# Low weight words scaled on GpSimd, a shorter warm-up and new priorities in a planned attention and two-MLP kernel

## The chip, the cores and the metric

The kernel runs on one core of a Trainium2 chip. The metric is the device time of one execution in microseconds (us). PE is TensorE, ACT is ScalarE, DVE is VectorE, POOL is GpSimd, and SP is the engine whose queue issues nearly all DMAs.

## What is computed

Windowed attention with a distance bias, then two MLPs on its 2304 output rows. All inputs are float32, but the four weight matrices reach the kernel as 64-bit numbers in 32-bit halves.

```python
scores = scale * q @ k.T + slopes * -|rel|     # 4 batches, 8 heads, 576 rows, head 64
scores = where(0 <= rel < 128, scores, -1e9)
x = softmax(scores) @ v                        # -> (2304, 512)
h = x @ w_in                                   # (2304, 2048)
P = a0 + a1*h + a2*h**2 + a3*h**3
Q = 1 + |b0|*|h| + |b1|*h**2
x = (P / (Q + 1e-6)) @ w_out                   # (2304, 512)
h = x @ w2_in
out = (h * sigmoid(h)) @ w2_out
```

## The kernel before

**A planner orders everything.** `plan_kernel` records each piece of work with `Plan.op`: a priority, an engine or a table of engines with a cost in ns for each, the tiles it reads and writes, and a function that issues it. `Plan.schedule` then plays the engines forward in time: of the pieces that are ready it takes the one of lowest priority, on the engine of its table where it can start first, and keeps tile buffers, DMA landings and the port that it lets POOL and DVE's SBUF operations share. The functions are called in the order of the planned start times; on the chip each engine runs its own part of that order and waits by semaphores. `OPT` holds the options (engines allowed for each kind of piece, offsets of priorities, numbers of buffers), and `SHIFTS` adds an offset to the priorities of stretches of pieces, by number.

**Attention.** The 18 tiles of 128 rows are cut into five blocks of 4, 4, 3, 4, 3 tiles. For each block and each of four pairs of heads a group (`group`, from L648 on) computes scores (L698) for two tiles at a time, a masked copy and bias and row minimum on DVE (L704, L711), exponentials on ACT (L715), a normalising product (L734, option `norm`, for block 0 `norm0`), transposes (L754), two masked halves `ph` of the transposed probabilities (on DVE at L799 and L803, or copied by ACT and masked by POOL at L785 and L786 in block 0; options `mk00` to `mk03` say which for the two heads of each group of block 0: `d` DVE, `p` POOL), and the product with v (L831). The result is split into a high word `xh` by a rounding copy and a low word `xl` by a subtraction (DVE at L855, or ACT and POOL at L851; options `xl00` to `xl03`).

**First MLP.** 80 steps of (block, 128 columns of 2048). A step computes `h` with 12 matmuls (L889 to L891: high by high, high by low, low by high, for four tiles of 128 rows of weights), the rational function on ACT and DVE (L905 to L934, the last one DVE's L934), its split into `gh` and `gl`, and 12 matmuls into four accumulators `acc` (L958 to L960).

**Weights.** Each of the 64 raw tiles (16 for each of the four matrices, 512 KB) goes through `raw_weight`: a load by SP into one of three buffers (L549); an ACT operation that rescales the top words (L561); the scaling of the low words in place, unsigned integers with a stride of two words, by 2^-32 × 7.499 (L564, option `shift`, on ACT in the kernel before); and a DVE shift and OR that joins the words (L567). `weight` then makes the high word (L466 or L474) and the low word (L485). First-MLP input weights are also written to DRAM (`spill`, L597, from the queue of option `sq`) and loaded again for later blocks (L606).

**Second MLP.** Three groups of six tiles by a fast matrix scheme with seven products; its weights are combined by `prep` (sums and splits, written to DRAM by SP, L1122) while the first MLP runs, and streamed back (L1133). Its matmuls are L1233 to L1235 and L1299 to L1301, all with 384 columns.

**The start.** `k_ident` makes an identity matrix on POOL; PE multiplies it with itself (`spin`, L511) `warm` times, and more often where the planner sees PE idle for over 300 ns before the first MLP runs. SP loads the first two tiles of k and q (L636), half of a table (L524), the next tiles, the other half, and so on.

Of the kernel before, what the change touches and what calls it, by code (L numbers as in the profile page):

```python
# [50 lines left out]
    'tabs': 'pool',  # L51
    'stb': 3,
    'strb': 3,
    'wpro': 0.256,
    'dS': -1.52,
    'dT': 0.037,
    'dA': 0.149,
    'dm': 0.366,
    'look': 0.451,
    'pw': -0.72,  # L60
    'pwo': -0.374,
    'dg': -5.616,
    'lead': 2.536,
    'slk': 0,
    'warm': 6,
    'fill': 0.6,
    'fillmin': 300.0,
    'fs': 10,
    'ob': 3,
    'pl': -0.721,  # L70
    'vlead': -1.233,
    'qlead': -1.974,
    'keen': 9999.0,
    'norm0': 'pool',
    'sq': 'act',
    'xq': 'sp',
    'mk': 'pd',
    'mk00': 'dd',
    'mk01': 'dp',
    'mk02': 'dd',  # L80
    'mk03': 'dd',
    'xl00': 'd',
    'xl01': 'd',
    'xl02': 'p',
    'xl03': 'd',
    'alt': 0,
    'gh0': 'act|dve',
    'gl0': 'pool',
    'la': 8.921,
    'lb': 302.617,  # L90
    'dm2': 1.231,
    'sums': 'pool',
    'fhi': 'act|pool',
    'flo': 'dve|pool',
# [1 line left out]
    'xsum': 'dve|pool',  # L96
    'xfh': 'act|pool',
    'xfl': 'pool',
    's1': 'act',
    'tsum': 'pool',  # L100
    'th': 'act|dve',
    'tl': 'dve|pool',
    'tlead': 1.016,
    'hlead': -0.505,
    'oq': 'sp',
    'pw2': 511.696,
    'rw2': 25.851,
    'pwo2': 1331.915,
    'rwo2': 14.569,
    'xlead': -0.854,  # L110
    'slead': 0.691,
    'shift': 'act',
    'tail': 1,
}

SHIFTS = [
# [6 lines left out]
]  # L125


# [44 lines left out]
class Plan:  # L172
# [11 lines left out]
    def op(self, prio, eng, cost, fn, reads=(), writes=(), after=(), dma=False):  # L184
# [6 lines left out]
        o.port = {e for e in o.alts if e == "pool" or e == "dve" and not o.banks}  # L191
        o.deps, o.allocs = set(after), []
        o.dma = dma or eng == "sp"
        o.lag = max([LAG.get(t[0], 0.0) for t in writes], default=0.0) if o.dma else 0.0
        for t in list(reads) + list(writes):
            key, reg = t[:2], t[2:]
            if key not in self.tile_ops:
# [191 lines left out]
def plan_kernel(ctx, tc, qn, kn, vp, table, w1, wo1, w2, wo2, out):  # L389
# [124 lines left out]
        T[("h", "spin")] = h_p.tile([P, 512], F32, tag="h", name="spin")  # L514
        spin(OPT["warm"])

    pl.op(-98, "pe", 427 * OPT["warm"], first_spin, reads=[("ident", 0)], writes=[("h", "spin")])
    pl.spin = spin

    late = []  # L520

    def late_consts():
        for part, cols in ((0, slice(0, 3 * P)), (1, slice(3 * P, 6 * P + 16))):
            pl.op(-91.0 + 0.5 * part, "sp", 700, lambda cols=cols: nc.sync.dma_start(tab_all[:, cols], table[:, cols]), writes=[("tab", part)])  # L524
        for part in range(2):
            for h in range(H):
                pl.op(-70 + 0.1 * h + 10 * (h // 2) + 25 * part, do_copy("act" if h + part == 0 else OPT["tabs"], 2 * P,
                      lambda h=h, part=part: (tabs[:, h, 2 * part:2 * part + 2], tab[:, 4 * part:4 * part + 2]), scale=-8.0 * 2.0 ** -(h + 1)), 0, None,
                      reads=[("tab", part)], writes=[("tabs", h, part)])
        late.append(("na", 0))  # L530
        late.append(("ab", 0))
        pl.op(-3, "dve", 80, lambda: nc.vector.tensor_scalar(out=na, in0=coef[:, 0:4], scalar1=-1.0, scalar2=None, op0=ALU.mult),
              reads=[("tab", 1)], writes=[("na", 0)])
        pl.op(-3, "act", 200, lambda: nc.scalar.activation(out=ab, in_=coef[:, 4:6], func=AF.Abs), reads=[("tab", 1)], writes=[("ab", 0)])
# [8 lines left out]
    def raw_weight(name, f, src, p, load_p):  # L543
# [12 lines left out]
        if wide:  # L556


            top = lambda: T[rk][:, :, 1].bitcast(F32)
            low = lambda: T[rk][:, :, 0].bitcast(U32)  # L560
            pl.op(p - 0.6, "act", c_act(NR) + 45, lambda: nc.scalar.activation(out=top(), in_=top(), func=AF.Prelu, scale=2.0 ** -112, alpha=2.0 ** 32),  # L561
                  reads=[rk + (1,)], writes=[rk + (1,)])
            pl.op(p - 0.5, any_of(OPT["shift"], {
                "act": (c_act(NR) + 45, lambda: nc.scalar.activation(out=low(), in_=low(), func=AF.Copy, scale=LOW_SCALE)),  # L564
                "dve": (c_dve2x(NR), lambda: nc.vector.tensor_scalar(
                    out=low(), in0=low(), scalar1=29, scalar2=None, op0=ALU.logical_shift_right))}), 0, None, reads=[rk + (0,)], writes=[rk + (0,)])
            pl.op(p - 0.3, "dve", c_dve(NR), lambda: nc.vector.scalar_tensor_tensor(  # L567
                out=top().bitcast(U32), in0=top().bitcast(U32), scalar=3, in1=low(), op0=ALU.logical_shift_left, op1=ALU.bitwise_or),
                reads=[rk], writes=[rk + (1,)])
# [890 lines left out]
```

## Time and profile before

| | us |
|---|---|
| median of 3 runs | 869.5 (868.25 to 870.54) |
| the profiled execution | 869.16 |
| its span, first to last instruction | 867.3 |
| PE busy | 855.2 (99%) |
| DVE busy | 643.1 (74%) |
| POOL busy | 637.9 (74%) |
| ACT busy | 603.1 (70%) |

Busy times add up the time in which an engine had an instruction in work. The ends of matmuls are modelled and overlap the next ones, so PE's busy time does not say how much of it is needed; the distance between the starts of matmuls does. A row of a timeline gives the start, the duration, the engine and line, what is written and read, and in brackets how long the engine was idle before it and what released it. A line of the chain of waits gives the start, the time spent and what it was spent on.

### The profile page before, as it was taken

Reading aid. Unit: us, or ns where it says so; the run is one execution under the profiler, and the core shown is the slowest. Engines: PE = TensorE matmul, PEld = TensorE weight load, DVE = VectorE, ACT = ScalarE, POOL = GpSimd, SP = SyncE. Lnnn points to the kernel's source line nnn. Section 1 sums busy time; section 2 is a strip of 40 time slices with the busy share of each in tenths; the row PEclk is TensorE's granted clock in tenths of the full one; section 3 lists DMA queues with packets and bytes.
Section 4 is the critical chain, followed back from the end, with each engine's and each line's share of the span. In section 5 each row is a group of like instructions: output and inputs, shape, how many; then the busy total and the mean of one; then the engine's idle time right before and its main releaser. Section 6 shows DMA issues by size and latency. Waiting matters only on the chain.

```text
span 867.3 us, 15300 instructions
## 1 busy us (share of the span) xinstructions
PE 855.2 (99%) x5076; PEld 765.1 (88%) x5076; DVE 643.1 (74%) x1308; ACT 603.1 (70%) x1291; POOL 637.9 (74%) x613
## 2 busy tenths in 40 slices
PE   8989999999999999999999999999999999999998
PEld 6667778877788998777889999999999999999998
DVE  7899897789999898998889984357733477433652
ACT  6699997799888988887889984446434365344452
POOL 4778845666888897878899677479954599744884
PEclk9999999999999999999999999999999999999999
DMA  7746764586889887876797889898888888878884
GB/s 253 264 161 214 243 223 137 169 277 227 289 310 321 294 280 263 306 255 238 275 349 240 295 297 356 262 318 281 281 277 250 292 288 282 295 248 258 252 269 169
DMA packets 80462, 228.94 MB, mean 264 GB/s; under 512 B 8192, under 2 KB 17152, under 8 KB 80384
## 3 DMA queue, kind: packets, MB, share of 16 engines
q1 hardware_dynamic: 78080, 219.59, 76.2%
q10 hardware_dynamic: 2304, 8.39, 2.4%
q8 instruction: 40, 0.66, 0.3%
q14 instruction: 38, 0.31, 0.1%
HBM read 178.66 MB, written 49.28 MB: 263 GB/s over the span
## 4 chain that ended last, share of the span: by engine, by line
PE 82%; DVE 5%; ACT 4%; POOL 3%; DMA 3%; issue 2%; SPq 0%; ACTq 0%; POOLq 0%; DVEq 0%
PE acc L958 6%; PE h L889 6%; PE acc L960 6%; PE acc L959 6%; PE h L891 5%; PE h L890 5%; PE z_a L1233 4%; PE z_b L1300 4%; PE z_a L1234 4%; PE z_a L1235 4%; PE z_b L1301 4%; PE z_b L1299 4%; PE bank_atA L831 3%; PE bank_atA L698 2%; PE bank_atA L1233 1%
## 5 line engine op out<-in xcount | busy, mean ns | idle before, releaser
L485 POOL TENSOR_TENSOR xl_b<-g,xh_b 128x384 fp32r<-128x384 f32 x81 | 90.6, 1119 | 69.6 <-ACT xh_b L466 67.8
L466 ACT CAST xh_b<-g 128x384 fp32r<-128x384 f32 x162 | 83.0, 514 | 64.3 <-PE z_b L1301 42.0
L958 PE MATMUL acc<-gh,wo 128*128 128x512 f32 (+1 forms) x320 | 121.1, 378 | 0.0
L960 PE MATMUL acc<-gl,wo 128*128 128x512 f32 (+1 forms) x320 | 118.7, 371 | 0.1
L959 PE MATMUL acc<-gh,wo 128*128 128x512 f32 (+1 forms) x320 | 117.8, 368 | 0.0
L481 DVE TENSOR_TENSOR xl_b<-g,xh_b 128x384 fp32r<-128x384 f32 x87 | 87.3, 1014 | 30.3 <-ACT xh_b L466 29.1
L485 POOL TENSOR_TENSOR gl<-t,gh 128x512 fp32r<-128x512 f32 (+1 forms) x76 | 93.0, 1224 | 15.9 <-ACT gh L466 12.5
L385 ACT ACTIVATE g<-t_a 128x384 f32<-128x384 f32 x72 | 37.9, 526 | 75.2 <-DVE t_a L378 75.2
L485 POOL TENSOR_TENSOR g<-g,g 128x384 f32<-128x384 f32 x72 | 84.5, 1185 | 2.0
L889 PE MATMUL h<-xh,ws 128*128 128x512 f32 (+1 forms) x224 | 84.2, 376 | 0.4 <-DVE t L934 0.4
L891 PE MATMUL h<-xh,ws 128*128 128x512 f32 (+1 forms) x224 | 82.2, 367 | 0.0
L890 PE MATMUL h<-xl,ws 128*128 128x512 f32 (+1 forms) x224 | 82.1, 367 | 0.0
L958 PEld LDWEIGHTS acc<-gh,wo 128*128 128x128 f32 x320 | 60.1, 188 | 13.4 <-issue 5.6
L960 PEld LDWEIGHTS acc<-gl,wo 128*128 128x128 f32 x320 | 60.0, 188 | 9.5 <-POOL gl L485 1.5
L959 PEld LDWEIGHTS acc<-gh,wo 128*128 128x128 f32 x320 | 60.1, 188 | 6.7
L1233 PE MATMUL z_a<-xf,w2s 128*128 128x384 f32 x192 | 64.2, 335 | 0.0
L1235 PE MATMUL z_a<-xf,w2s 128*128 128x384 f32 x192 | 64.1, 334 | 0.0
L1234 PE MATMUL z_a<-xf,w2s 128*128 128x384 f32 x192 | 64.1, 334 | 0.0
L1299 PE MATMUL z_b<-xh_b,wo2s 128*128 128x384 f32 x192 | 64.1, 334 | 0.0
L1300 PE MATMUL z_b<-xl_b,wo2s 128*128 128x384 f32 x192 | 64.1, 334 | 0.0
L1301 PE MATMUL z_b<-xh_b,wo2s 128*128 128x384 f32 x192 | 64.1, 334 | 0.0
L715 ACT ACTIVATE e<-e,m 128x128 f32<-128x128 f32 x144 | 56.0, 392 | 7.6 <-DVE m L711 7.3
(207 smaller groups left out, 2701.9 us busy)
## 6 DMA issues: line engine op xcount, KB each, us to landing
w2s<-forms_w SPq DMA_DIRECT2D x84, 512.0 KB, 4.7
wo2s<-forms_wo SPq DMA_DIRECT2D x84, 512.0 KB, 4.6
ws<-sc SPq DMA_DIRECT2D x64, 512.0 KB, 4.4
raw_w<-in_w SPq DMA_DIRECT2D x32, 512.0 KB, 4.9
raw_wo<-in_wo SPq DMA_DIRECT2D x32, 512.0 KB, 4.9
forms_w<-st_w SPq DMA_DIRECT2D x24, 512.0 KB, 5.0
forms_wo<-st_wo SPq DMA_DIRECT2D x24, 512.0 KB, 4.9
sc<-w ACTq DMA_DIRECT2D x16, 512.0 KB, 5.2
```

Source lines behind the costliest of these rows:

```text
L485: nc.gpsimd.tensor_tensor(out=o, in0=a, in1=b, op=op)
L889: nc.tensor.matmul(o, lhsT=T[W][:, 0, c], rhs=xh, start=kt == 0, stop=False)
L890: nc.tensor.matmul(o, lhsT=T[W][:, 0, c], rhs=xl, start=False, stop=False)
L891: nc.tensor.matmul(o, lhsT=T[W][:, 1, c], rhs=xh, start=False, stop=kt == KD - 1)
L958: nc.tensor.matmul(a, lhsT=T[WO][:, 0, c], rhs=T[G1][:, :n], start=first_f, stop=False)
L959: nc.tensor.matmul(a, lhsT=T[WO][:, 1, c], rhs=T[G1][:, :n], start=False, stop=False)
L960: nc.tensor.matmul(a, lhsT=T[WO][:, 0, c], rhs=T[G2][:, :n], start=False, stop=last_f)
L1233: nc.tensor.matmul(o, lhsT=w(0, kt * P), rhs=x[:, 0, kt], start=st and kt == 0, stop=False, skip_group_check=True)
L1234: nc.tensor.matmul(o, lhsT=w(0, kt * P), rhs=x[:, 1, kt], start=False, stop=False, skip_group_check=True)
L1235: nc.tensor.matmul(o, lhsT=w(1, kt * P), rhs=x[:, 0, kt], start=False, stop=kt == 1, skip_group_check=True)
L1299: nc.tensor.matmul(o, lhsT=w(0, m * P), rhs=h, start=st and q == 0, stop=False, skip_group_check=True)
L1300: nc.tensor.matmul(o, lhsT=w(0, m * P), rhs=l, start=False, stop=False, skip_group_check=True)
```

## The change

Low words may now be scaled by POOL as well as ACT; the planner gives POOL 46 of the 64. The warm-up is three matmuls, not six, and is planned at 470 ns each. Spills go to SP's queue. The planner no longer adds a delay of its own after the first q, k, v and table loads, and takes more time for the table. Normalising in block 0 may go to DVE, several pieces get one more engine, the masks and low words of single groups of block 0 change engines, and the offsets of priorities and `SHIFTS` are new numbers throughout.

```diff
-    'warm': 6,
+    'warm': 3,
-    'vlead': -1.233,
-    'qlead': -1.974,
+    'vlead': 0.616,
+    'qlead': 0.725,
-    'norm0': 'pool',
-    'sq': 'act',
+    'norm0': 'dve|pool',
+    'sq': 'sp',
-    'mk00': 'dd',
-    'mk01': 'dp',
+    'mk00': 'pd',
+    'mk01': 'dd',
-    'xl00': 'd',
-    'xl01': 'd',
-    'xl02': 'p',
+    'xl00': 'p',
+    'xl01': 'p',
+    'xl02': 'd',
-    'gh0': 'act|dve',
-    'gl0': 'pool',
+    'gh0': 'act',
+    'gl0': 'dve|pool',
-    's1': 'act',
+    's1': 'act|dve',
-    'th': 'act|dve',
+    'th': 'act|dve|pool',
-    'shift': 'act',
+    'shift': 'act|pool',
...
 SHIFTS = [
...
-        o.lag = max([LAG.get(t[0], 0.0) for t in writes], default=0.0) if o.dma else 0.0
+        o.lag = max([LAG.get(t[0], 0.0) for t in writes if t[1] != 0], default=0.0) if o.dma else 0.0
...
-    pl.op(-98, "pe", 427 * OPT["warm"], first_spin, reads=[("ident", 0)], writes=[("h", "spin")])
+    pl.op(-98, "pe", 470 * OPT["warm"], first_spin, reads=[("ident", 0)], writes=[("h", "spin")])
...
-            pl.op(-91.0 + 0.5 * part, "sp", 700, lambda cols=cols: nc.sync.dma_start(tab_all[:, cols], table[:, cols]), writes=[("tab", part)])
+            pl.op(-91.0 + 0.5 * part, "sp", 1150, lambda cols=cols: nc.sync.dma_start(tab_all[:, cols], table[:, cols]), writes=[("tab", part)])
...
             pl.op(p - 0.5, any_of(OPT["shift"], {
                 "act": (c_act(NR) + 45, lambda: nc.scalar.activation(out=low(), in_=low(), func=AF.Copy, scale=LOW_SCALE)),
+                "pool": (c_pool_ts(NR) + 90, lambda: nc.gpsimd.tensor_scalar(out=low(), in0=low(), scalar1=LOW_SCALE, scalar2=1.0, op0=ALU.mult, op1=ALU.mult)),
```

The other numbers of `OPT` that change are offsets of priorities: `wpro`, `dS`, `dT`, `dA`, `dm`, `look`, `pw`, `pwo`, `dg`, `lead`, `pl`, `la`, `lb`, `dm2`, `tlead`, `hlead`, `pw2`, `rw2`, `pwo2`, `rwo2`, `xlead`, `slead`. `SHIFTS` has 60 entries in place of 37.

## Rows read from the trace of the kernel before

**Rows 1.** Busy time by stretch: PE, PEld, DVE, ACT, POOL, clock, DMA, GB/s.

```profile
0.00:57.00 57.00, 49.92 (x447) 36.59 (x447) 47.03 (x179) 41.55 (x135) 37.55 (x50) 1.00 0.71 239
57.00:520.00 463.00, 461.24 (x2647) 384.76 (x2648) 416.20 (x884) 406.26 (x849) 361.03 (x360) 1.00 0.76 260
520.00:867.30 347.30, 344.02 (x1985) 343.70 (x1983) 179.83 (x246) 155.28 (x308) 239.36 (x204) 1.00 0.84 274
```

**Rows 2.** The same view, of two stretches with matmuls of one width.

```profile
140.00:150.00 10.00, 10.00 (x46) 8.29 (x45) 7.88 (x15) 6.72 (x10) 5.38 (x6) 1.00 0.33 107
560.00:580.00 20.00, 20.00 (x117) 20.00 (x117) 9.23 (x15) 8.08 (x16) 11.41 (x12) 1.00 0.94 309
```

**Rows 3.** Timeline of PE: transposes, values, a wait for h, a scores block.

```profile
25.57 1.09 PE L754 MATMUL bank_acc<-ident,e 128*128 128x128 f32 x8
...
50.25 1.95 PE L831 MATMUL bank_atA<-ph,vh 128*64 128x256 f32 x20 [1.27 <-POOL ph L792]
...
54.52 0.50 PE L889 MATMUL h<-xh,w 128*128 128x512 f32 x1 [1.01 <-DVE t L934]
...
56.11 0.37 PE L698 MATMUL bank_atA<-kd,qd 64*64 64x192 f32 x1
...
56.92 0.50 PE L889 MATMUL h<-xh,w 128*128 128x512 f32 x1
```

**Rows 4.** Instructions of the spin line: duration ns min/median/max, first and last start.

```profile
L511 PE MATMUL spin<-ident x62: 275/275/582, 1.4 to 27.3; 128*128 128x128 f32 x62
...
L511 PE MATMUL bank_acc<-ident x38: 272/275/377, 30.7 to 53.2; 128*128 128x128 f32 x38
```

**Rows 5.** Timeline of the first 7 us, and the landing of k's loads up to 12 us.

```profile
1.17 0.42 SPq L636 DMA_DIRECT2D qd<-in_qn  x1
...
1.36 3.78 PE L511 MATMUL spin<-ident 128*128 128x128 f32 x16 [1.36 <-POOL ident masks.py:199]
...
4.47 0.42 ACT L466 ACTIVATE tabs<-tab 128x256 f32<-128x256 f32 x1 [2.46 <-DMA tab<-in_table]
...
5.07 0.57 PE L698 MATMUL bank_atA<-kd,qd 64*128 64x128 f32 x1
...
6.30 0.29 DVE L704 COPY_PREDICATED bank_atA<-tab,bank_atA 128x128 f32<-128x128 uint32 x1 [2.11 <-PE bank_atB L698]
...
DMA to landing us min/median/max: 2.2/4.1/8.3
```

**Rows 6.** The chain that ended last, in the first 62 us.

```profile
12.00 2.05 POOL e L734 x2
...
25.63 1.24 POOL ph L785
...
26.95 1.28 POOL ph L786
...
34.23 6.79 DMA raw_w<-in_w
...
43.80 0.56 ACT raw_w L564
```

**Rows 7.** DVE's joining of words: least/median/most; then its group (busy, mean ns).

```profile
L567 DVE SCALAR_TENSOR_TENSOR raw_w<-raw_w x32: 647/736/1404, 20.3 to 360.7; 128x512 uint32<-128x512 uint32 x32
...
L567 DVE SCALAR_TENSOR_TENSOR raw_w<-raw_w 128x512 uint32<-128x512 uint32 x32 | 26.2, 824 | 1.9 <-ACT raw_w L564 1.7
```

**Rows 8.** Instructions of the low-word scaling on ACT (32 more on raw_wo).

```profile
L564 ACT ACTIVATE raw_w<-raw_w x32: 647/672/703, 17.6 to 357.2; 128x512 uint32<-128x512 uint32 x32
```

**Rows 9.** Groups of POOL up to 520 us: busy, mean ns of one, idle before.

```profile
L485 POOL TENSOR_TENSOR w<-raw_w,w 128x512 fp32r<-128x512 f32 x16 | 21.4, 1338 | 0.9 <-ACT w L466 0.2
...
L474 POOL TENSOR_SCALAR wo<-raw_wo 128x512 fp32r<-128x512 f32 x11 | 7.6, 690 | 12.9 <-DVE raw_wo L567 12.9
```

**Rows 10.** Waits of DVE: us in total, times, longest us.

```profile
DVE t L930 <- ACT h L928: 19.5, 30, 2.5
```

**Rows 11.** Timeline of POOL and DVE at 28 us.

```profile
28.18 1.30 POOL L485 TENSOR_TENSOR w<-raw_w,w 128x512 fp32r<-128x512 f32 x1
...
28.40 1.11 DVE L726 TENSOR_SCALAR l<-l 128x8 f32<-128x8 f32 x1 [0.24 <-ACT e L715]
```

**Rows 12.** Spills on ACT's queue, and SP's waits before raw loads.

```profile
L597 ACTq DMA_DIRECT2D sc<-w x16: 326/326/362, 24.7 to 195.8; - x16
...
SPq L549 <- POOL w L485: 46.9, 15, 5.8
```

More of the change, by code (lines that the diff above doesn't have):

```diff
@@ L53 @@
     'strb': 3,
[L54 to L63, printed above, removed]
+    'wpro': 0.226,
+    'dS': -1.459,
+    'dT': 0.01,
+    'dA': 0.283,
+    'dm': 0.426,
+    'look': 0.312,
+    'pw': -0.595,
+    'pwo': -0.37,
+    'dg': -1.781,
+    'lead': 2.551,
     'slk': 0,
-    'warm': 6,
+    'warm': 3,
     'fill': 0.6,
@@ L69 @@
     'ob': 3,
-    'pl': -0.721,
-    'vlead': -1.233,
-    'qlead': -1.974,
+    'pl': -0.649,
+    'vlead': 0.616,
+    'qlead': 0.725,
     'keen': 9999.0,
-    'norm0': 'pool',
-    'sq': 'act',
+    'norm0': 'dve|pool',
+    'sq': 'sp',
     'xq': 'sp',
     'mk': 'pd',
-    'mk00': 'dd',
-    'mk01': 'dp',
+    'mk00': 'pd',
+    'mk01': 'dd',
     'mk02': 'dd',
     'mk03': 'dd',
-    'xl00': 'd',
-    'xl01': 'd',
-    'xl02': 'p',
+    'xl00': 'p',
+    'xl01': 'p',
+    'xl02': 'd',
     'xl03': 'd',
     'alt': 0,
-    'gh0': 'act|dve',
-    'gl0': 'pool',
-    'la': 8.921,
-    'lb': 302.617,
-    'dm2': 1.231,
+    'gh0': 'act',
+    'gl0': 'dve|pool',
+    'la': 7.958,
+    'lb': 108.335,
+    'dm2': 4.831,
     'sums': 'pool',
@@ L98 @@
     'xfl': 'pool',
-    's1': 'act',
+    's1': 'act|dve',
     'tsum': 'pool',
-    'th': 'act|dve',
+    'th': 'act|dve|pool',
     'tl': 'dve|pool',
-    'tlead': 1.016,
-    'hlead': -0.505,
+    'tlead': -0.003,
+    'hlead': -0.973,
     'oq': 'sp',
[L106 to L111, printed above, removed]
-    'shift': 'act',
+    'pw2': 30.726,
+    'rw2': 16.788,
+    'pwo2': 1188.783,
+    'rwo2': 3.36,
+    'xlead': -0.899,
+    'slead': 0.222,
+    'shift': 'act|pool',
     'tail': 1,
```

15 rows, old and new, of the table SHIFTS are left out of this document.

## Prediction

> **What bounds the kernel now.** I read the busy times by stretch first. They fall into three stages [rows 1]. From 520 us to the end PE is busy without a break, and DVE, ACT and POOL have half their time or more to spare but for POOL (239 of 347 us). Nothing that only relieves or loads those three can move the end of that stage: it is 2,016 matmuls of 384 columns one after another. From 57 to 520 us PE is again busy (461.2 of 463 us), but DVE (416), ACT (406) and POOL (361) are nearly full. From 0 to 57 us PE is busy for 49.9 us, partly with idle spins.
>
> How much of this is lost is worked out from the spacing of matmuls, since their modelled ends hide short pauses. Where only matmuls of 512 columns run, 46 are counted in 10 us with both edges in, which makes about 0.225 us each; with 384 columns 117 in 20 us make 0.172 us [rows 2]. By the code the first MLP has 48 steps of 24 matmuls with 512 columns and 32 steps of 24 with 384: 259 + 132 us. The second MLP takes 2,016 × 0.172 = 347 us. The attention of 72 tile pairs: a scores block of two tiles takes 56.92 - 56.11 = 0.81 us, so 72 × 0.4 = 29 us; a transpose about 0.12 us, 144 of them 17 us; the values 1.95 us for a group of four tiles and about three quarters of it for one of three, together 35 us [rows 3]. The sum is some 819 us, an estimate good to a few us. The span is 867.3 us, so some 48 us are not work. About 26 us of them lie in the first 57: the 100 spin records [rows 4], 16 at 0.23 us and the others at about 0.12, make some 14 us, and PE's waits and starts between them, such as the waits of about 1 us before 50.25 and 54.52 us [rows 3], most of the rest. Some 15 to 20 us are left for 57 to 520 us, as pauses of about 0.1 us where a block of matmuls begins. These two sums are all that the change can win from.
>
> **The start.** Six warm-up matmuls become three. The 16 spin records from 1.36 us on end when the first scores matmul starts at 5.07 us; by the code they are six warm-up matmuls and two fillers, of two records each. The first q was issued at 1.17 us, and the quickest landing of these loads took 2.2 us, so the data were there at about 3.4 us [rows 5]. Three warm-up matmuls fewer are six records of about 0.22 us, 1.3 us, so the scores can start at about 3.8 us. DVE's first operation on them then comes at about 5.0 us, after the table's landing (ACT's first use of it was released at 4.47 us), in place of 6.30 [rows 5]. That 1.3 us is the gain if nothing else is late, and nothing is gained if the next groups' q and k, which land as before, end the wait. The new leads for q, k and v (qlead -1.97 to 0.73, vlead -1.23 to 0.62) put those loads ahead of raw weights in SP's queue, which helps the groups and delays the weights. I take **-0.9 us**, between 0 and -1.3 and nearer the full gain because the chain passes from these spins straight into group 0. The later rise of TensorE's clock has a price: the first spins run at half the later rate (16 records in 3.78 us against 8 in 1.09 us at 25.57 of the same size [rows 3, 5]), which is the lower of 1.2 and 2.4 GHz although the column shows 1.00 there. If the rise comes later by the 1.3 us of spins that are gone, the work in it takes twice as long, at most +0.7 us; that end stays in the range.
>
> **The attention of block 0.** Normalising may now go to DVE too. On the chain it is 2.05 us at 12.00 [rows 6] for two POOL operations; the DVE scores operations around it are each 0.2 to 0.4 us, and a DVE product of 512 elements costs some 0.65 us by its nearest row (L567's least, 0.65 [rows 7]), 1.3 us for the pair: -0.7 us where DVE is free. Group 1's masks go from ACT and POOL to DVE: the two POOL pieces at 25.63 and 26.95 (2.5 us on the chain) become about 1.3 us: -1.2 us. Group 0's go the other way for one head, +1.2 us by the same prices, but beside the other head's masks on DVE, so I count half. Groups 0 and 1 get their low words from POOL (an extra ACT copy and 1.3 us of POOL), group 2 from DVE; for the price of two DVE operations saved and one added I count nothing, with ±1 us as bounds. Sum **-1.3 us**; bounds -3 and +2.
>
> **The shift.** Each low-word scaling on ACT takes 0.67 us, 0.56 us of it on the chain where operations stand back to back [rows 6, 8]. On POOL it does not exist in this trace. The nearest row is POOL's one-input copy from the same strided raw tile, 0.69 us; the far end is POOL's two-input operation, 1.34 us [rows 9]. I take 0.69 since the new operation has one input. So 46 of them take 46 × 0.56 = 26 us from ACT and put 32 us (up to 62) on POOL. In the first stage ACT is the chain without a break from 41 to 50 us, with one scaling in it, and POOL idles before 44 us: **-0.6 us**, or up to -1.7 with the two other scalings of that stretch. From 57 to 520 us ACT falls to about 383 of 463 us and POOL rises to about 390. What ends PE's pauses there is DVE's last operation of a step, and DVE in turn waits for ACT (19.5 us at L930 alone [rows 10]); with ACT 6% emptier I let these waits shrink by a tenth and a tenth of the 15 to 20 us go with them: -1.7 us.
>
> Against that stands DVE's wait for POOL. A DVE operation of 8 elements took 1.11 us at 28.40, until POOL's operation of 28.18 had ended [rows 11], and L567 takes 0.65 us at best, 1.40 at worst and 0.82 in the mean [rows 7]. The excess of 0.17 us over 64 of them is 11 us; with 9% more POOL work it grows by 1 us, some of it hidden: +0.5 us. Net for the stage **-1.2 us**. The Trainium skill says in "SBUF — State Buffer", Who interferes with whom, that GpSimd and DVE instructions with two SBUF inputs hold a shared port pair exclusively for a whole instruction, and that ScalarE waits for nobody. The two rows agree, and by that rule the move puts 32 us of new lock where ACT had none. Taken at full price it is the second rival below.
>
> **The rest.** Spills move from ACT's queue to SP: 16 issues of 0.33 us [rows 12], which overlap ACT's work now. SP already waits for the same POOL operation before a raw load (15 times, 46.9 us), so a spill beside it delays a load by 0.33 us: nothing, covered by load times of some 5 us. If a spill stood ahead of a load that was ready, the load would be late by SP's wait, up to 5.8 us [rows 12]; one such case reaching PE costs about 1 us. Splits and copies of the second MLP, which get POOL or DVE as a further choice, lie under a PE without gaps: nothing. In block 0 the high words of g leave DVE for ACT and the low words may come to DVE: one copy each way, inside the bounds that follow. The new priorities and shifts of whole stretches have no row. Their bounds are half of the pauses gone (-8 us) and five waits of the size before 54.52 (+5 us); I take 0 beyond what is counted.
>
> **Sum.** -0.9 - 1.3 - 0.6 - 1.2 = -4.0 us. The profiled execution took 869.16 us (span 867.3), 0.3 us under the median of 869.5. 869.2 - 4.0 = 865.2 us. About 0.3%, 2.6 us, is what a measurement here can tell from no change: below 866.9 is faster, above 872.1 slower.
>
> **Rivals.** (a) Hidden anyway: the first stage ends where weight loads (6.8 us for the one at 34.23 [rows 6]) and DVE (47 of 57 us) let it, and 57 to 520 us is matmul-bound to within 0.1 us pauses that come from semaphores and not from late engines. Then only a few tenths of the start remain: 868.9 us. For it: PE is 99.6% busy there; against it: the spins. Chance 0.25. (b) Slower, by the port: POOL's scalings hold off DVE at full price. From 57 to 520 us DVE has 463 - 416 = 47 us free. If half of the 46 push back a DVE operation by their length, DVE loses 23 × 0.69 = 16 us; half of that reaches PE, +8 (I choose the middle between none and all), and only the first stage's gains stay: 869.2 - 2.8 + 8 = 874.4. It decides once DVE exceeds about 430 us in that stage. Against it: a scaling can be put where DVE works on PSUM alone. Chance 0.19. (c) More than counted: mask, normalising and scaling gains add up in the first stage (-5), and a quarter of the pauses go (-4): 860.5 us. Chance 0.14. The forecast keeps 0.42.
>
> **How the numbers follow.** Faster: (c) and all but a sliver of the forecast, 0.55. Same: (a) and that sliver, 0.26. Slower: (b), 0.19. The likeliest case alone spans 862 to 867.5. The range from 859.5 to 872.6 takes in (a), most of (c) and the lowest quarter of (b), which I let run from 872.1 to 880; some 18 in 100 are left out.
>
> **What would show it.** Scores start near 3.8 us; about 18 of L564 are left on ACT and 46 stand on POOL at 0.65 to 0.75 us; steady matmuls begin 2 to 3 us earlier, before 55 us; ACT is busy about 25 us less up to 520 us; L567's mean stays under 0.9 us; the last stage is 347 us long as before. The prediction is wrong if the start's gain is gone by 57 us, if POOL's scaling takes over 1 us, or if DVE's busy time before 520 us grows by over 15 us.

## The result and the profile after

The changed kernel takes 874.81 us, median of four runs (874.3 to 876.31), against 869.23 us before in the same comparison (868.25 to 870.54): ratio 1.0059, interval 1.0045 to 1.0073. It is slower, by 5.6 us; 4 us less than before was forecast. The profiled execution took 876.31 us with a span of 874.5, which is 7.2 us over the span before, more than the medians differ, since it is the slowest of the four.

Busy time of the changed kernel in the first two stretches, columns as in [rows 1]:

```profile
0.00:57.00 57.00, 50.42 (x440) 37.42 (x440) 48.38 (x180) 39.07 (x130) 43.29 (x56) 1.00 0.69 227
57.00:520.00 463.00, 457.08 (x2623) 377.89 (x2622) 424.23 (x889) 387.77 (x805) 362.02 (x372) 1.00 0.74 255
```

ACT was relieved as planned: 387.8 us in the middle stage against 406.3 [rows 1]. POOL was given 46 scalings, 40 of them in this stage, yet its busy time there stands at 362.0 against 361.0. DVE's went up from 416.2 to 424.2. So in this stage POOL gave about as much work away as it took, and DVE got part of it. Over the whole span POOL is busy 24.5 us longer (662.4 against 637.9) and DVE 20.6 us (663.7 against 643.1). The second MLP takes as long as before and starts later: the n-th matmul of the last stage is 7.2 us later than the same one before from 520 us to the end.

The work that went over, as groups of instructions of the kernel before up to 530 us (busy us, mean ns of one, idle time before them):

```profile
L485 POOL TENSOR_TENSOR gl<-t,gh 128x512 fp32r<-128x512 f32 x48 | 63.6, 1324 | 13.1 <-ACT gh L466 10.2 <-DVE gh L470 2.0
L485 POOL TENSOR_TENSOR st_wo<-sums_wo,st_wo 128x512 fp32r<-128x512 f32 x15 | 20.2, 1348 | 1.9 <-ACT st_wo L466 1.4
```

and the same view of the kernel after:

```profile
L488 POOL TENSOR_TENSOR gl<-t,gh 128x512 fp32r<-128x512 f32 x40 | 52.4, 1310 | 7.3 <-ACT gh L469 5.4
L488 POOL TENSOR_TENSOR st_wo<-sums_wo,st_wo 128x512 fp32r<-128x512 f32 x8 | 10.4, 1302 | 1.7 <-ACT st_wo L469 1.5
...
L484 DVE TENSOR_TENSOR gl<-t,gh 128x512 fp32r<-128x512 f32 x8 | 8.9, 1118 | 1.1 <-ACT gh L469 1.1
L484 DVE TENSOR_TENSOR st_wo<-sums_wo,st_wo 128x512 fp32r<-128x512 f32 x6 | 6.9, 1157 | 0.9 <-DMA w2s<-forms_w 0.9
```

Eight splits of `gl` and seven of `st_wo` left POOL, one operation of 1.3 us for about every three scalings of 0.67 that came. Eight of the first and five of the second are new on DVE (it had one `st_wo`). How dear they are there stands in the instructions of DVE's split line (least, median, most ns; first and last start):

```profile
L484 DVE TENSOR_TENSOR gl<-t,gh x12: 559/984/1520, 99.6 to 524.6; 128x512 fp32r<-128x512 f32 x8, 128x384 fp32r<-128x384 f32 x4
```

**Where the time is lost.** The delay of the n-th matmul against before, taken from the starts of both traces, is 1.1 us at 66 us, 4.2 at 340, 5.0 from 427 to 445, 6.9 from 450 to 457 and 7.2 at 520. It is not one place. The waits of PE that the profile names (us in total, times, longest), first of the kernel before, then of the kernel after:

```profile
PE h L889 <- DVE t L934: 2.6, 3, 1.2
...
PE h L893 <- DVE t L938: 4.5, 6, 1.6
...
PE acc L964 <- POOL gl L488: 1.1, 2, 0.6
```

Before, PE waited three times and 2.6 us for the last DVE operation of a step; the wait of 1.01 us in [rows 3] is one of them. Now it waits six times and 4.5 us. Two of the six, 0.89 us until 428.84 and the longest, 1.59 us until 451.94, follow from these pieces of the chain that ended last (start us, us, what):

```profile
424.80 1.48 DVE st_wo L484
426.27 0.60 DVE t L934
...
428.19 0.61 DVE t L938
428.84 0.50 PE h L893
...
447.63 1.87 DVE xs L484
```

Two splits, 1.48 and 1.87 us, stand directly ahead of the step operations that PE waits for. The timeline of DVE from 445 us on, and then rows of POOL, show why they are so long:

```profile
445.45 1.52 DVE L484 TENSOR_TENSOR gl<-t,gh 128x512 fp32r<-128x512 f32 x1
446.90 0.74 DVE L928 SCALAR_TENSOR_TENSOR t<-t,na,h 128x512 f32<-128x512 f32 x1
447.55 1.95 DVE L484 TENSOR_TENSOR xs<-xf,xs 128x768 f32<-128x768 f32 x1
...
424.71 1.01 POOL L796 TENSOR_TENSOR ph<-ph 128x384 f32<-128x384 f32 x1
...
445.56 0.87 POOL L477 TENSOR_SCALAR xf<-xf 128x768 fp32r<-128x768 f32 x1
446.52 2.17 POOL L488 TENSOR_TENSOR xf<-xf 128x768 fp32r<-128x768 f32 x1
448.65 2.55 POOL L488 TENSOR_TENSOR xf<-xs,xf 128x768 fp32r<-128x768 f32 x1
```

While these splits run, POOL has operations of its own in work. The `gl` split at 445.45 takes 1.52 us where the least of the eight of 512 columns is 0.68 (the 0.56 above is one of 384 columns), the `xs` split 1.95. How long a split is held can be read off. When that at 424.80 began, POOL's operation of 424.71 still had 0.93 us to run; the split took that and 0.55 us more. Sixteen of the eighteen splits of 512 columns that DVE has up to 533 us follow this sum, the rest of the running POOL operation and 0.54 to 0.58 us; one that met no POOL operation took 0.69, and that at 445.45 let a second POOL operation pass as well. In the Trainium skill, "SBUF — State Buffer", Who interferes with whom, a DVE instruction with two SBUF inputs contends with a GpSimd instruction that reads SBUF, for a port pair that one of them holds exclusively. The stretched splits agree with it. The step operation at 446.90, which by the code takes `h` from PSUM and so has one SBUF input, took 0.74 us with POOL in work as well: not every overlap stretches.

On the whole chain DVE's share went from 5% to 14%. In experiment 11, which lost more, it is 7%, so the share alone is no measure of a loss.

The scalings themselves are as cheap as forecast, 0.67 us by the median and 32.5 us in all on POOL. Their instructions on POOL and the 18 left on ACT:

```profile
L568 POOL TENSOR_SCALAR raw_w<-raw_w x25: 652/666/1211, 14.1 to 364.3; 128x512 uint32<-128x512 uint32 x25
L568 POOL TENSOR_SCALAR raw_wo<-raw_wo x21: 649/667/1177, 44.0 to 525.3; 128x512 uint32<-128x512 uint32 x21
...
L567 ACT ACTIVATE raw_wo<-raw_wo x11: 652/672/695, 33.4 to 497.5; 128x512 uint32<-128x512 uint32 x11
L567 ACT ACTIVATE raw_w<-raw_w x7: 659/668/681, 21.2 to 318.2; 128x512 uint32<-128x512 uint32 x7
```

**The start.** The timeline of PE, and DVE's first operation on the scores, answer to [rows 5]:

```profile
1.36 2.08 PE L514 MATMUL spin<-ident 128*128 128x128 f32 x8 [1.36 <-POOL ident masks.py:199]
3.54 0.55 PE L702 MATMUL bank_atA<-kd,qd 64*128 64x128 f32 x1
...
5.12 2.01 PE L514 MATMUL spin<-ident 128*128 128x128 f32 x8
5.24 0.29 DVE L708 COPY_PREDICATED bank_atA<-tab,bank_atA 128x128 f32<-128x128 uint32 x1 [1.05 <-PE bank_atB L702]
```

The first scores start at 3.54 us in place of 5.07 and DVE at 5.24 in place of 6.30. But at 5.12 the fillers come, eight records in 2.01 us. In the kernel before the eight took 1.16, and the second half of the scores followed them:

```profile
6.18 1.16 PE L511 MATMUL spin<-ident 128*128 128x128 f32 x8
7.31 0.54 PE L698 MATMUL bank_atA<-kd,qd 64*64 64x192 f32 x2
```

The second half now starts at 7.06 against 7.31, and by 66 us the matmuls are late. The trace's record of the granted clock begins, at the higher level, at 6.94 us in this trace and at 5.51 us in that of before. Ahead of it there is no record, and the clock column counts that as 1.00.

### The profile page after: what moved, and what is told of

It is laid out like the page before. It is cut to its first block, busy times and chain, and to the rows that moved or that the text cites. A ratio compares the mean times of both kernels' runs of the same rounds, so it can differ in the third digit from the quotient of the medians.

```text
span 874.5 us, 15327 instructions
## 1 busy us (share of the span) xinstructions
PE 858.7 (98%) x5086; PEld 766.1 (88%) x5086; DVE 663.7 (76%) x1331; ACT 573.7 (66%) x1222; POOL 662.4 (76%) x660
## 4 chain that ended last, share of the span: by engine, by line
PE 71%; DVE 14%; ACT 6%; DMA 3%; POOL 3%; issue 3%; SPq 0%; ACTq 0%; POOLq 0%; DVEq 0%
PE acc L962 4%; PE h L893 4%; PE h L895 4%; PE h L894 4%; PE acc L964 4%; PE acc L963 4%; PE z_b L1305 4%; PE z_b L1303 4%; PE z_b L1304 4%; PE z_a L1239 4%; PE z_a L1237 4%; PE z_a L1238 4%; DMA forms_w<-st_w 2%; PE bank_atA L835 2%; PE bank_atA L702 2%
## 5 line engine op out<-in xcount | busy, mean ns | idle before, releaser
L469 ACT CAST xh_b<-g 128x384 fp32r<-128x384 f32 x135 | 69.3, 515 | 64.7 <-PE z_b L1305 43.9
L488 POOL TENSOR_TENSOR gl<-t,gh 128x512 fp32r<-128x512 f32 (+1 forms) x68 | 83.3, 1225 | 11.0 <-ACT gh L469 8.4
L964 PEld LDWEIGHTS acc<-gl,wo 128*128 128x128 f32 x320 | 60.0, 188 | 10.9 <-POOL gl L488 2.7
```

The lines of the kernel that those rows point to most:

```text
L488: nc.gpsimd.tensor_tensor(out=o, in0=a, in1=b, op=op)
L964: nc.tensor.matmul(a, lhsT=T[WO][:, 0, c], rhs=T[G2][:, :n], start=False, stop=last_f)
```

## The experiments

Two theories stood at the start, Theory 1 and Theory 2 of the first expectations, here T1 and T2. T1: POOL's scalings hold off DVE, so that without them the time of before comes back. T2: the new order as a whole, its priorities and the choice of engines for other pieces, is the loss, and the scalings are only one of its pieces. To tell them apart the planned order must not move with the edit. In the kernels called "held" the planner runs as in its kernel, and then only what is issued in a place of its plan is changed. In their diffs, `scale` stands for the pieces whose engine became POOL by the option `shift`, picked out of the plan after `schedule`. Each ratio is to the kernel before, run beside it on the same chip (its median 869.2 to 870.0). Executions of one kernel differ by 1 to 4 us, and a ratio is known to 0.001 to 0.002 either way, some 1 to 2 us.

**1. The order after, the 46 scalings issued by ACT in the same places.**

```diff
 pl.schedule(...)
+for o in scale:
+    o.fn = o.alts["act"][1]
```

> The changed kernel with its planned order kept as it is; only the 46 scalings that POOL issues are issued by ACT at the same places. Theory 1 (the loss comes from the place of the scalings: 32 us more on POOL, which holds DVE off and pushes its splits to DVE): 869 to 872 us. Theory 2 (the loss comes from the new order of work, whoever scales): 874 to 877 us, since ACT gets 26 us more.

Measured: 878.52 us (878.25 to 879.62), ratio 1.0105 (1.0090 to 1.0120). Above both expectations: in an order made for POOL, the scaling on ACT is 3.7 us dearer than on POOL (878.5 - 874.8). ACT does matter where the plan counts on it to be free, so this edit can't say what the scalings on POOL cost. T1 in the form that undoing the move brings back the time falls.

**2. The order after, the 46 scalings left out.** The joins read a tile of zeros, so that the low words drop out of all 64 weights and the joins wait for no scaling.

```diff
+zero = const.tile([P, 1], U32, name="zero")
...
-    out=top().bitcast(U32), in0=top().bitcast(U32), scalar=3, in1=low(), ...
+    out=top().bitcast(U32), in0=top().bitcast(U32), scalar=3, in1=zero.broadcast_to([P, DM]), ...
...
+for o in scale:
+    o.fn = lambda: None
```

> The changed kernel with its planned order kept; the 46 scalings on POOL are left out and the joining operation reads zeros in place of the low words, so the lowest three bits of each weight are missing. Theory 1: 867 to 870 us, all of the loss comes back. Theory 2: 873 us or more, within 2 us of the changed kernel.

Measured: 872.54 us (871.64 to 874.99), ratio 1.0037 (1.0021 to 1.0053). In the order after, the scalings cost 874.8 - 872.5 = 2.3 us of the 5.6, an amount that is itself known to some 2 us only (the intervals of the two ratios overlap). The other 3.3 us are there without a single scaling on POOL.

**3. The order after, each of POOL's scalings issued twice,** first by 1.0, then by the real factor.

```diff
-"pool": (..., lambda: nc.gpsimd.tensor_scalar(..., scalar1=LOW_SCALE, ...))
+"pool": (..., lambda: (nc.gpsimd.tensor_scalar(..., scalar1=1.0, ...), nc.gpsimd.tensor_scalar(..., scalar1=LOW_SCALE, ...)))
```

> The changed kernel with its planned order kept; each of the 46 places on POOL issues two scalings (the first by 1.0, so that up to 24 leading bits of the low word stay). Theory 1: another 32 us on POOL cost at least what the first did, 880 us or more. Theory 2: 875 to 877 us, because POOL's operations are mostly early enough.

Measured: 885.1 us (884.01 to 886.36), ratio 1.0179 (1.0164 to 1.0194). The second set costs 10.3 us, the first 2.3. In the waits of PE the split behind the scalings on POOL's own queue now comes first; before the doubling this wait stood at 1.1 us in two times:

```profile
PE acc L964 <- POOL gl L488: 6.0, 7, 1.6
```

So the price of a POOL operation is not its length but what stands behind it. The plan seems to have left room for one scaling each, not for two.

**4. The order after, with about the old engines:** the scalings on ACT as in 1, and the 18 splits of 512 columns that DVE has before 530 us given to POOL. In the kernel before DVE had four such splits, so POOL gets four more than it had.

```diff
+for o in scale:
+    o.fn = o.alts["act"][1]
+for o in split:
+    o.fn = o.alts["pool"][1]
```

> The changed kernel with its planned order kept; the 46 scalings go to ACT and the 18 subtractions of 512 elements that DVE took over before 530 us go back to POOL, so that each engine has about the work that it had before, in the new order. Theory 1: 868 to 871 us. Theory 2: 873 to 876 us.

Measured: 883.23 us (882.65 to 886.08), ratio 1.0164 (1.0146 to 1.0181). Putting the loads of the engines about where they were makes it worse still: the engines can't be undone without the order.

**5. The order after, the 18 splits on DVE replaced** by a memset of the same tile, which reads nothing; the low words of these pieces are zero.

```diff
+for o in split:
+    o.fn = o.fn.zero        # nc.vector.memset(o.bitcast(F32), 0.0)
```

> The changed kernel with its planned order kept; the 18 subtractions of 512 elements that DVE does before 530 us (low words of g and of weight sums) are replaced at their places by DVE writing zeros, an operation of nearly the same length that reads nothing and so waits for no POOL operation. The low words concerned are zero. Theory 3 (the loss comes from DVE's own splits, which POOL's longer use of the port holds up with a step's chain queued behind them): 870 to 872 us, and PE's waits for DVE's L938 near 428 and 450 us are gone. Rival (the order is late whatever holds the port): 874 to 875 us.

Theory 3 is new here: DVE's own splits, held up by POOL, are the loss. Measured: 872.83 us (872.38 to 874.55), ratio 1.0043 (1.0028 to 1.0058): about 2.0 us of the loss hang on these splits, part of it perhaps because a memset is shorter (0.485 us against 0.69 for a split that nothing held). All of them took the same time, whatever POOL did (least, median, most ns of the eight of `gl`; the other ten too), and in the waits of PE the step's is smaller:

```profile
L492 DVE MEMSET gl<- x8: 485/485/485, 98.5 to 443.6; 128x512 f32 x8
...
PE h L899 <- DVE t L944: 2.8, 5, 1.0
```

The 4.5 us are down to 2.8. The wait near 428 us is gone; the one near 449 is 0.98 us, since the `xs` split of 768 columns ahead of it was not among the 18. This shows the mechanism of the two chain pieces above.

**6. The order after, the spills issued from ACT's queue** as before.

```diff
-queue(OPT["sq"]).dma_start(scratch[f], T[wk].bitcast(F32))
+nc.scalar.dma_start(scratch[f], T[wk].bitcast(F32))
```

> The changed kernel with its planned order kept; the 16 spills are issued from ACT's queue at the same places instead of SP's. If spills hold up the loads behind them on SP in the first stage: 873 to 874.3 us and steady matmuls up to 1.5 us earlier at 57 us. Rival (SP waits there anyway): 874.8 us, within 0.5.

Measured: 874.76 us (874.04 to 876.25), ratio 1.0063 (1.0048 to 1.0078), the time of the changed kernel. The queue of the spills costs nothing that can be told.

**7. The old options in the planner after:** its new figures for the warm-up, the table and the first loads, three warm-ups, and all other options and `SHIFTS` as before.

```diff
-OPT = { ...after... }
+OPT = { ...before..., 'warm': 3 }
-SHIFTS = [ ...after... ]
+SHIFTS = [ ...before... ]
```

> The changed kernel's planner (its figures for the first loads, the table and the warm-up) with three warm-ups, but all other options, priorities and shifts of the kernel before, planned again. If the earlier start is worth what it moves: 867 to 868.5 us. Rival (the start is hidden by later landings, and a new plan that was not searched is no better): 869 to 873 us.

Measured: 870.22 us (869.8 to 871.17), ratio 1.0007 (0.9997 to 1.0017): no change. So the planner's new figures and the shorter warm-up neither gain nor lose by themselves, and the loss comes with the options and the priorities.

**8. The kernel before, held, with three warm-ups.**

```diff
-spin(OPT["warm"])
+spin(OPT["warm"] // 2)
```

> The kernel before with its planned order kept, three warm-up matmuls issued instead of six. If the first scores' start is on the path: 868 to 868.7 us. Rival (hidden by the landings of the next groups' q and k, or given back by TensorE's later clock): 869.0 to 870 us.

Measured: 869.17 us (868.14 to 870.24), ratio 0.9995 (0.9984 to 1.0006). No gain clear of noise; the interval alone would leave room for the 0.9 us of the forecast. The timeline of PE shows where the 1.3 us went:

```profile
1.36 2.50 PE L511 MATMUL spin<-ident 128*128 128x128 f32 x10 [1.36 <-POOL ident masks.py:199]
3.79 0.58 PE L698 MATMUL bank_atA<-kd,qd 64*128 64x128 f32 x1
...
5.37 2.07 PE L511 MATMUL spin<-ident 128*128 128x128 f32 x8
7.37 0.37 PE L698 MATMUL bank_atA<-kd,qd 64*64 64x192 f32 x1
```

The scores start 1.28 us earlier (3.79 against 5.07). From there to the fillers it takes 1.58 us where it took 1.11, and the eight filler records take 2.07 us where they took 1.16, so that the second half starts at 7.37 against 7.31. What was taken off the warm-up is paid back by slower matmuls. The trace's record of the clock begins at 7.37 us here and at 5.51 before; a scores matmul of 192 columns took 0.52 to 0.58 us ahead of it and 0.32 to 0.37 from there on. In the traces of this case it begins at 4.80 to 6.02 us in the three kernels with six warm-ups and at 5.95 to 10.39 us in the twelve with three. PE is at work from 1.35 or 1.36 us on in all of them.

**9. Both cuts, 2 and 5, in the order after.**

```diff
+for o in split:
+    o.fn = o.fn.zero
+for o in scale:
+    o.fn = lambda: None
```

> The changed kernel with its planned order kept; both earlier cuts together: the 46 scalings on POOL are left out (joins read zeros) and the 18 subtractions on DVE before 530 us are replaced by DVE writing zeros. If port traffic is all of the loss (each cut alone gave 2.0 to 2.3 of 5.6 us): 869 to 870.8 us. Rival (about half of the loss is in the order itself, and the two cuts relieve the same waits): 871.5 to 873 us.

Measured: 873.82 us (872.38 to 874.2), ratio 1.0044 (1.0027 to 1.0060). The cuts don't add up: 2.3 and 2.0 us apart, about 1 us together, where the sum of 4.3 would have given 870.5. That both relieve the same overlaps of POOL and DVE is likely, and not shown. With neither the scalings nor the 18 splits there, the order after is still 3 to 4 us slower than before. Two waits of PE in the profiled execution are part of that: 1.04 us until 447.86, behind an `xs` split of 768 columns that the edit left in place, and 1.28 us until 496.09 for a `gl` split on POOL:

```profile
443.01 2.41 DVE L484 TENSOR_TENSOR xs<-xf,xs 128x768 f32<-128x768 f32 x1
...
447.86 0.44 PE L901 MATMUL h<-xh,ws 128*128 128x384 f32 x1 [1.04 <-DVE t L946]
...
496.09 0.44 PE L972 MATMUL acc<-gl,wo 128*128 128x384 f32 x1 [1.28 <-POOL gl L488]
```

The kernel before has the same split at 446.32; it took 1.22 us there, and PE did not wait behind it. The delay against before grows from 1.5 us at 445 to 2.8 at 450 and 4.2 at 500, and is 3.3 from 520 on.

**10. POOL's planning costs set to what the trace shows,** and the options after planned with them.

```diff
-return 149 + 2.1 * n
+return 202 + 2.13 * n
...
-return 160 + 0.836 * n + 83 * aps
+return 190 + 0.836 * n + 83 * aps
```

> The changed kernel with one thing changed in its planner: POOL's two-input operations are planned at 202 ns + 2.13 ns for each element and its one-input operations at 190 + 0.836, as the traces show them (1.29 us for 512 elements), in place of 149 + 2.1 and 160 + 0.836; options and priorities as they are, planned again. If the chip falls behind the plan because POOL is planned too short: first late matmuls of the second MLP less than 10 us behind their planned start (16.7 in the changed kernel, 11.3 in the kernel before), at a total of 873 to 878 us, since the priorities were not searched for these costs. Rival (the drift has another cause): 14 us or more behind its plan, 880 us or more.

Measured: 889.05 us (888.3 to 891.47), ratio 1.0222 (1.0203 to 1.0242). The idea behind it: the plan promised 858.0 us for the kernel after and 856.3 for the one before, and on the chip the second MLP's matmuls at 600 us lag behind their planned starts by 16.6 and 11.2 us. If too low a cost for POOL made the difference, true costs should shrink the lag. It went to 14.3 us only. That doesn't settle it: the new plan, 869.5 us long, gives POOL 41 scalings and DVE 13 of the splits of 512 columns, in place of 46 and 18, since `SHIFTS` were fitted to another plan. Its waits are longer, and after the longest the granted clock was 0.50 for 3.4 us, by which some 1.7 us are lost (an estimate, half of the stretch). PE's waits, the matmul behind the longest, and the busy times of that stretch:

```profile
PE h L893 <- DVE t L938: 8.4, 8, 3.3
...
132.91 0.50 PE L893 MATMUL h<-xh,ws 128*128 128x512 f32 x1 [3.29 <-DVE t L938]
...
133.80:137.20 3.40, 3.40 (x10) 2.65 (x9) 1.55 (x6) 0.99 (x4) 2.80 (x3) 0.50 0.01 2
```

**11. The kernel before, held, with the same 46 scalings issued by POOL.** `ON_POOL` lists the tiles that POOL scales in the kernel after.

```diff
-"act": (..., lambda: nc.scalar.activation(out=low(), in_=low(), ...))
+"act": (..., (lambda: nc.gpsimd.tensor_scalar(out=low(), in0=low(), ...)) if rk[1] in ON_POOL else (lambda: nc.scalar.activation(...)))
```

> The kernel before with its planned order kept; the scalings of the same 46 raw tiles as in the changed kernel are issued by POOL at the places where ACT did them, and nothing else is changed: the first item of the change alone. If POOL's extra 32 us and the port are what costs: 874 us or more. If the loss is a matter of the new order around them: 868.5 to 871.5 us.

Measured: 882.39 us (880.94 to 882.7), ratio 1.0143 (1.0128 to 1.0159), 12.4 us more than the kernel before beside it. It is the change's main part alone. Its middle stage by busy times:

```profile
57.00:520.00 463.00, 453.20 (x2581) 373.15 (x2581) 410.45 (x867) 379.34 (x791) 382.49 (x390) 1.00 0.75 252
```

PE's longest wait in total:

```profile
PE h L890 <- DVE t L935: 4.5, 6, 1.2
```

and DVE's joins in that stage, first before and then here (the last column: DVE idle just before them, and for whom):

```profile
L567 DVE SCALAR_TENSOR_TENSOR raw_wo<-raw_wo 128x512 uint32<-128x512 uint32 x31 | 25.3, 817 | 2.4 <-ACT raw_wo L564 2.2
L567 DVE SCALAR_TENSOR_TENSOR raw_w<-raw_w 128x512 uint32<-128x512 uint32 x27 | 22.8, 847 | 1.9 <-ACT raw_w L564 1.7
...
L568 DVE SCALAR_TENSOR_TENSOR raw_wo<-raw_wo 128x512 uint32<-128x512 uint32 x29 | 26.6, 918 | 7.2 <-POOL raw_wo L565 5.9 <-ACT raw_wo L565 1.4
L568 DVE SCALAR_TENSOR_TENSOR raw_w<-raw_w 128x512 uint32<-128x512 uint32 x27 | 25.3, 939 | 10.9 <-POOL raw_w L565 10.9
```

The new cost is not only the port. The joins' means rise from 817 and 847 ns to 918 and 939, about 0.1 us for each, but DVE also stands idle 18.1 us ahead of them (7.2 + 10.9), 16.8 of it for POOL's scaling, where it stood idle 4.3 before. Each of the 46 scalings started right behind another operation of POOL, so it had waited its turn in POOL's queue. DVE's operations run one after another in the planned order, so the step operations behind a join wait with it.

In the kernel after, the same groups show next to none of this wait:

```profile
L571 DVE SCALAR_TENSOR_TENSOR raw_w<-raw_w 128x512 uint32<-128x512 uint32 x27 | 23.9, 886 | 2.1 <-ACT raw_w L564 1.6 <-POOL raw_w L568 0.5
L571 DVE SCALAR_TENSOR_TENSOR raw_wo<-raw_wo 128x512 uint32<-128x512 uint32 x28 | 22.2, 792 | 1.1 <-issue 0.6 <-POOL raw_wo L568 0.4
```

The new order has the scalings early enough and has made room on POOL by giving splits to DVE; the scalings that cost 12.4 us in the old order cost 2.3 in this one. The kernel as a whole didn't get back to where the kernel before stood.

**12 and 13. Two orders searched anew,** with the costs of experiment 10: one from the options before, with all scaling on ACT; one from the options after, with scaling on POOL or ACT. Beside the two cost lines of experiment 10 only `OPT` and `SHIFTS` change.

```diff
-OPT = { ...after... }; SHIFTS = [ ...after... ]
+OPT = { ...found by the search... }; SHIFTS = [ ...found by the search... ]
```

> The changed kernel's planner with POOL's corrected costs and priorities searched again from the old ones for these costs; scalings stay on ACT (new numbers, engines of single pieces and shifts; three warm-ups). Its plan is 9 us shorter than that of the old options under the same costs. If chip and plan part by about as much as for the kernel before: 861 to 866 us, faster than both kernels. Rival (a searched order always falls further behind its plan, as the changed kernel did by 5 us): 866 to 870 us.

> The same, searched from the changed kernel's options, with scalings free to go to POOL; its plan is 8 us shorter than that of the changed options under these costs. If scaling on POOL is harmless in an order that was searched with POOL's true costs: 863 to 868 us. If the port makes it lose whatever the order: 871 us or more.

Measured: 877.05 us (876.38 to 878.6), ratio 1.0088 (1.0073 to 1.0103), and 879.5 us (878.05 to 880.93), ratio 1.0108 (1.0088 to 1.0127). Each search had gained 8 to 9 us on paper, and both lost on the chip; the lag behind the plan at 600 us was 15.9 and 15.6 us. Neither beats the kernel before, and neither does any other version here. The first lost most in one place: its profiled execution is 1.4 us behind the kernel before at 500 us and 7.1 behind at 520. There the second MLP starts while a write of its combined weights to DRAM is on the chain (5.79 us from 513.69), PE waits 3.1 us, and then the granted clock is 0.50 for 3.4 us:

```profile
PE bank_atA L1223 <- DVE t_a L367: 3.1, 1, 3.1
```

**14. The kernel before, held, with the same 46 scalings left out.** The joins read zeros as in 2, so the low words drop out.

```diff
-"act": (..., lambda: nc.scalar.activation(out=low(), in_=low(), ...))
+"act": (..., (lambda: None) if rk[1] in ON_POOL else (lambda: nc.scalar.activation(...)))
```

> The kernel before with its planned order kept; the scalings of the same 46 raw tiles are left out on ACT and given to no engine (all joins read zeros, so the lowest three bits of each weight are missing). This is what relieving ACT of 26 us is worth when nobody pays for it. The step of the prediction on ACT's relief (0.6 us in the first stage, 1.7 us after it): 867 to 868 us. Rival (ACT was early enough; the chain of a step waits for DVE and POOL): 869 to 870.5 us.

Measured: 870.17 us (868.71 to 871.9), ratio 1.0004 (0.9993 to 1.0015). This is the best that the move could bring in that order: ACT without the scalings, POOL without them too. It brings nothing, or 0.6 us at the far end of the interval. Its middle stage by busy times:

```profile
57.00:520.00 463.00, 460.46 (x2651) 383.64 (x2644) 419.12 (x883) 386.76 (x806) 359.85 (x359) 1.00 0.76 259
```

and the wait of DVE that answers to [rows 10]:

```profile
DVE t L933 <- ACT h L931: 19.0, 28, 2.8
```

ACT is 19.5 us emptier (406.3 - 386.8), and DVE waits for it 19.0 us in place of 19.5. The wait is the step's own: DVE hands `h` to ACT and needs it back. A freer ACT didn't return it sooner.

## Why the prediction was wrong

The forecast was -4.0 us, and +5.6 was measured, outside its range. (The range ended at 872.6, which takes in a sixteenth of rival (b)'s stretch from 872.1 to 880 and not the quarter that the text names; a quarter would have ended at 874.1.) The start's gain was gone by 57 us, which was one of its signs of being wrong.

**The shift, -1.2 us: wrong in sign.** The step that failed is "with ACT 6% emptier I let these waits shrink by a tenth and a tenth of the 15 to 20 us go with them: -1.7 us". ACT did get that much emptier, and experiment 14 measured the worth of it in the old order: nothing, where this and the first stage's -0.6 make 2.3. I took a wait for ACT as a sign of a busy ACT. The kernel after shows the trap well: there the DVE wait for ACT did shrink, from 19.5 us in 30 times to

```profile
DVE t L934 <- ACT h L932: 13.8, 21, 1.2
```

by more than the forecast tenth, and the kernel is slower. The other half, "+0.5 us" for the port, was mis-sized: the scalings cost 2.3 us in the new order and 12.4 in the old one. The price I put on them counted DVE's stretched joins, and not that a join also waits for POOL's queue (16.8 us in experiment 11), nor that POOL's splits would go elsewhere: POOL was to rise to about 390 us in the middle stage, stands at 362, and DVE's new splits cost some 2 us (experiment 5). One of the two rows that stand beside the rule of the shared port pair, [rows 11], is no case of two SBUF inputs: that operation has one, and was held all the same.

**The priorities, "0 beyond what is counted": wrong.** They were put at nothing because no row gave a price. With scalings and DVE's splits of 512 columns both cut out, 3 to 4 us of loss stay (experiment 9), and the planner's figures and warm-up are not it (experiment 7). The search had gained 0.6 us on paper (858.65 to 858.04, from the options of experiment 7 to those after) and lost 874.8 - 870.2 = 4.6 on the chip. The bounds of -8 and +5 held, the value between them didn't.

**The start, -0.9 us: 0.** Scores and DVE started when forecast (3.54 us and 5.24 against about 3.8 and 5.0). The step that failed is "nearer the full gain because the chain passes from these spins straight into group 0". It does, but the group's second half stands behind scores and fillers that run at the lower clock level for longer. That was the "+0.7 us" of the clock, named and left as an end of the range, and it was too small: the fillers alone lost 0.85 to 0.9 us (2.01 and 2.07 against 1.16), the first scores about 0.5 more.

**Block 0's attention, -1.3 us, and the first stage's -0.6: not seen.** The matmuls are 1.1 us later at 66 us, not 2 to 3 earlier. These two were not tried by themselves; in the profiled execution this stage holds 1.1 of the 7.2 us.

**Right:** 46 scalings on POOL and 18 on ACT, 0.67 us by the median where 0.69 was taken; spills at nothing (experiment 6); the last stage's length unmoved; DVE under its sign of failure, 9.4 us more before 520 us where over 15 was set. L571's means of 886 and 792 ns also stayed under 0.9 us. These signs are of single operations, and the loss lies in the waits between them.

**The rival that came nearest** is (b), slower by the port. Its 874.4 us is the time measured, but by half of its mechanism: DVE reached 424 us, below the 430 at which it was to decide, and the loss came through displaced splits and order rather than through scalings at full price. Its agreement in time is partly chance.

**Open.** What in the new order costs the 3 to 4 us that stay in experiment 9 was found in part only: some 1.3 us come with the `xs` split that no edit touched, and the rest lies in short pauses that were not told apart. Single options, such as the engines of block 0's masks, were not tried alone. What makes the plan optimistic by 11 to 17 us is open too; experiment 10 doesn't tell how much of it is POOL's cost.

## What to carry to other kernels

Before moving work off an engine, leave that work out and time the kernel: if the emptier engine brings nothing in that order, the move can only cost there. Price an operation given to an in-order engine by what then stands behind it and who waits for that, not by its length, and ask what the planner will push off that engine in return. A searched plan's gain on paper is worth nothing while it is smaller than the change in the lag between plan and chip: here 0.6 us was gained and 4.6 lost.

## What was not expected of the hardware

The same 46 operations of 0.67 us cost 12.4 us in one order of the queues and 2.3 in another, and doubling them in the second cost 10.3 more. A DVE split with two SBUF inputs that began while a POOL operation ran took the rest of that operation and 0.54 to 0.58 us, in sixteen of seventeen cases; a memset in its place took 0.485 us each time. Behind a shorter warm-up the lower clock level reaches further: the eight filler records took 2.01 to 2.07 us instead of 1.16, and with the slower scores ahead of them this gave back all of the 1.28 us that three warm-up matmuls had taken, though the clock column shows 1.00 where the trace has no record of the clock yet.
